# Batch start of a fused attention and feed-forward kernel: who splits the second and third pair, when reciprocals are taken, and when the first batch's value products run

## The chip, the cores and the metric

The kernel runs on one core of one Trainium2 chip. The core has five engines, each with an instruction queue of its own that is worked off in order: TensorE (PE, matrix products and transposes), VectorE (DVE), ScalarE (ACT), GpSimd (POOL) and SyncE (SP, which only starts transfers). The metric is the device time of one execution in microseconds, lower is better. Times are medians over several executions; a profile shows one further execution.

## What is computed

For 8 batches and 8 heads with 576 positions and head size 64, attention with a threshold below the row's largest score, then a feed-forward layer with a leaky rectifier on the joined heads:

```python
scores = scale * np.matmul(q, k.transpose(0, 1, 3, 2))
thresh = np.max(scores, axis=-1, keepdims=True) - tau
scores = np.where(scores >= thresh, scores, -1000000000.0)
scores = scores - np.max(scores, axis=-1, keepdims=True)
attn = np.exp(scores)
attn = attn / (np.sum(attn, axis=-1, keepdims=True) + 1e-09)
attn_out = np.matmul(attn, v)
x = attn_out.transpose(0, 2, 1, 3).reshape(B * S, H * D)
h = x @ w_in                      # 4608 x 512 by 512 x 2048
out = np.maximum(0.01 * h, h) @ w_out
```

## The kernel before

**Steps.** The work of attention is cut into 144 steps, 18 for each batch (`PERB`). A step holds 128 queries of a pair of heads against all 576 keys. The 512 main positions of a batch give two blocks, each of four pairs of heads by two halves `c`; two further steps hold the 64 tail positions of all heads. Two steps (`c` 0 and 1) of the same pair make a `Pair`, whose weights are turned and multiplied with the values together. The first 8 steps are called `early`: their weights are turned on TensorE (`turn_w_pe`), those of all others by a transposing transfer on SyncE's queue (`turn_w`).

**One step.** `scores` (L244) makes the scores of both heads on TensorE into one pair of PSUM tiles `sc`, and there is only one such pair, so that the next step's scores wait for `copy_min`. `copy_min` (L252, VectorE) copies the negated scores out and takes the row minimum. `threshold` adds tau (L261 on VectorE up to step 27, L264 on GpSimd from there). One step later `exps` (ScalarE, L283, L284, L287) makes the exponentials, and `weights` (L296, VectorE) the thresholded weights of head 0. `recip` (L302, VectorE) inverts the sums, `widen` (L305) spreads the result beside the weights so that it is turned along with them. `pv` (L340, TensorE) multiplies turned weights with the values some steps later, `evacuate` (L362 and L352, VectorE) scales and stores the result as input `x` of the layers. It, `pv` and the filler products share one PSUM buffer, "pv". Four pairs make a group of 256 tokens, whose `layer1` units (L383) run one for each step and `layer2` units (L399) two for each step.

**Splitting.** Queries and keys are needed as two half-precision parts, turned so that the head size lies on the partitions. A key such as `(0, 1, "k")` names batch, pair and tensor; `"t"` in place of the pair is the tail. `split_now` rounds to the first part on ScalarE (L157) and takes the rest on VectorE (L158). `split_pool` does all of it on GpSimd: `split_scale` (L137), `split_high` (L143), `split_low` (L147). `turn` (L176) transposes both parts on TensorE into a PSUM tile of the two buffers called "h", and a copy (L187, tails L179 and L184) moves them to SBUF. The buffers for split parts, `half`, are four.

**Order.** The order of the instructions is written out by hand: the loop at the end goes through the steps `n`, and what is put in `loads_at`, `turns_at`, `pool_at`, `rows_at` and `pv_at` is issued at its step, at the place in the step that the loop has. `first` is the list of the first batch's units: pair 0 keys and queries, tail keys, pair 1 keys (`first[3]`) and queries (`first[4]`), pair 2 keys and queries (`first[5]`, `first[6]`), pair 3 keys and queries, tail queries. Pair 0 and the tail keys are split by `split_now` ahead of the loop, pair 1 by `split_now` in step 0, the others by `split_pool`. `idle` (L505) issues filler products on TensorE. Products with the values follow `pv_at`: three steps after the pair's second step where it is early, four in the first batch, five elsewhere. Layer weights are loaded and converted by transfers on GpSimd's queue (`load_w`, L489 and L492).

Of the kernel before, what the change touches and what calls it, by code (L numbers as in the profile page):

```python
# [10 lines left out]
FP16 = mybir.dt.float16  # L11
AX = mybir.AluOpType
# [25 lines left out]
def kernel(  # L38
# [43 lines left out]

    def load_tails(b, which, eng=None):
        t = sb.tile([128, 2, 2, 64], FP32, tag="rawt", bufs=2, name="rawt")
        src = SRC[which][b, :, MAIN:S, :].rearrange("(u sh) p d -> u p sh d", u=2)
        for u in range(2):
            (eng or nc.sync).dma_start(out=t[ds(64 * u, 64), :, :, :].rearrange("p s h d -> p (s h) d"), in_=src[u])
        tails[b, which] = t
# [55 lines left out]

    def split_low(key):
        n = 2 if key[1] == "t" else 4
        nc.gpsimd.tensor_tensor(out=halves[key][:, 1, 0:n, :, :], in0=scaled.pop(key)[:, 0:n, :, :],  # L147
                                in1=halves[key][:, 0, 0:n, :, :], op=AX.subtract)

    def split_now(key):  # L150
        t = halves[key] = new_half()
        for i in range(2):
            if key[1] == "t":
                src, n = tails[key[0], key[2]][:, :, i, :], 2
            else:
                src, n = pair_of(*key)[:, i, :, :], 4
            nc.scalar.activation(out=t[:, 0, 0:n, i, :], in_=src, func=AF.Copy, bias=0.0, scale=64.0)  # L157
            nc.vector.scalar_tensor_tensor(out=t[:, 1, 0:n, i, :], in0=src, scalar=64.0, in1=t[:, 0, 0:n, i, :],  # L158
                                           op0=AX.mult, op1=AX.subtract)

    def turn(key, copy=None):
        copy = copy or nc.scalar.copy
# [14 lines left out]
        if p == "t":  # L177
            for x in range(2):
                copy(out=dst[:, x, :, ds(c0, 64)], in_=tp[:, x, :, :, :].rearrange("d u s p -> d (u s) p"))  # L179
            if which == "k" and b:  # L180
                nc.gpsimd.tensor_copy(out=dst[:, :, :, 576:640], in_=dst[:, :, :, 0:64])
            elif which == "k":
                for x in range(2):
                    nc.vector.tensor_copy(out=dst[:, x, :, 576:640],  # L184
                                          in_=tp[:, x, :, :, :].rearrange("d u s p -> d (u s) p"))
        else:
            copy(out=dst[:, :, p, ds(c0, 512)], in_=tp[:, :, :, :].rearrange("d x t p -> d x (t p)"))  # L187
# [283 lines left out]
    load_pair(0, "q", nc.scalar)  # L471
    load_tails(0, "k", nc.sync)
    load_pair(1, "k", nc.sync)
# [4 lines left out]
    for s in range(2):  # L478
        load_v(0, s)
        if s == 0:  # L480
            load_vtails(0)
    load_tails(0, "q", nc.sync)
    for t in v16:
# [133 lines left out]
```

## Time and profile before

| | us |
|---|---|
| median of 3 runs | 500.47 (500.11 to 500.74) |
| profiled execution | 500.9 |
| its span in the profile | 499.1 |
| TensorE busy | 475.7 (95% of the span) |
| ScalarE busy | 433.1 (87%) |
| VectorE busy | 414.3 (83%) |
| GpSimd busy | 305.5 (61%) |

The span runs from the first to the last instruction; the execution's time has a little around it. Busy times of engines overlap. In a timeline a row is start, duration, engine, line of the kernel, operation, tiles written and read, shape, and in brackets the idle time ahead of it with what ended it. "SPq" and "ACTq" are the queues that start transfers, and "PEld" is TensorE's loading of stationary operands beside its products.

### The profile page before, as it was taken

How to read it: one execution, taken by the hardware profiler on the slowest of the kernel's cores; microseconds unless marked ns; L12 is line 12 of the kernel's file. 1: busy time of each engine (PE TensorE's matmuls, PEld its weight loads, DVE VectorE, ACT ScalarE, POOL GpSimd, SP SyncE). 2: the span in 40 equal slices, each digit the busy share in tenths (PEclk: the TensorE clock that was granted, in tenths of full speed). 3: DMA queues.
4: the chain of work that ended last, by engine and by line, in shares of the span. 5: the costliest groups of instructions: out<-in, count | busy, mean ns of one | idle time of the engine just before them, and what ended most of it. 6: DMA issues, size and time to landing. Idle time of an engine off the chain costs nothing.

```text
span 499.1 us, 19695 instructions
## 1 busy us (share of the span) xinstructions
PE 475.7 (95%) x8043; PEld 344.4 (69%) x8043; DVE 414.3 (83%) x1228; ACT 433.1 (87%) x785; POOL 305.5 (61%) x517
## 2 busy tenths in 40 slices
PE   7878789989999999999999999999999999999996
PEld 6556566656677777777777777777777777667884
DVE  4999999998989898998989898998989898878100
ACT  4998987898999999999999999999999999999431
POOL 4973687557867687666867687666867683322000
PEclk9989999999999999999999999999999999999999
DMA  8897898899998999999997999999898969767512
GB/s 246 238 202 121 156 193 175 144 205 189 217 168 182 193 204 211 186 165 220 191 185 172 203 199 199 195 172 210 197 200 153 205 148 158 138 117 144 126 45 65
DMA packets 220443, 87.79 MB, mean 176 GB/s; under 512 B 190656, under 2 KB 217280, under 8 KB 220352
## 3 DMA queue, kind: packets, MB, share of 16 engines
q1 hardware_dynamic: 217392, 82.07, 80.5%
q0 software_dynamic: 2688, 4.19, 4.8%
q8 instruction: 63, 1.03, 0.9%
q10 hardware_dynamic: 272, 0.26, 0.2%
q14 instruction: 28, 0.23, 0.1%
HBM read 36.70 MB, written 9.44 MB: 92 GB/s over the span
## 4 chain that ended last, share of the span: by engine, by line
PE 80%; DVE 11%; ACT 3%; DMA 2%; issue 1%; POOL 1%; SPq 0%; DVEq 0%; POOLq 0%; ACTq 0%
PE hp L383 26%; PE o L399 20%; PE sc L244 20%; PE pv L340 7%; DVE s L252 5%; PE osc L399 3%; DVE w L296 3%; PE tpr L199 3%; DMA wT<-w 2%; DMA rawt<-in_k_dram 1%; DVE x L362 1%; ACT wT L325 1%; ACT s L283 1%; DVE half L158 1%; ACT e L287 1%
## 5 line engine op out<-in xcount | busy, mean ns | idle before, releaser
L252 DVE TENSOR_SCALAR_CACHE_REDUCE s<-sc 128x576 f32<-128x576 f32 x288 | 206.4, 754 | 32.6 <-PE sc L244 31.4
L244 PE MATMUL sc<-kT,qT 64*128 64x288 f16 (+1 forms) x1920 | 135.8, 286 | 4.0 <-DVE s L252 3.2
L383 PE MATMUL hp<-x,win 128*64 128x256 f16 x2048 | 136.5, 275 | 1.1 <-DVE x L362 1.0
L383 PEld LDWEIGHTS <-win 128*64 128x64 f16 x2560 | 118.5, 109 | 24.0 <-issue 18.1
L399 PE MATMUL o<-wout,g 128*64 128x512 f16 x992 | 127.8, 379 | 0.0
L296 DVE SCALAR_TENSOR_TENSOR w<-s,th,e 128x576 f16<-128x576 f32 x144 | 122.2, 849 | 0.5 <-ACT e L287 0.5
L244 PEld LDWEIGHTS <-qT 64*128 64x128 f16 (+1 forms) x1920 | 77.0, 97 | 58.6 <-issue 44.2
L264 POOL TENSOR_SCALAR th<-mn 128x2 f32<-128x2 f32 x116 | 53.5, 461 | 103.3 <-DVE s L252 76.9
L284 ACT ACTIVATE w<-s,minus_tau 128x576 f16<-128x576 f32 x144 | 111.7, 776 | 5.2
L283 ACT ACTIVATE s<-s,th 128x576 f32<-128x576 f32 x144 | 110.4, 766 | 2.0 <-POOL th L264 1.4
L287 ACT ACTIVATE e<-s,mn 128x576 f16<-128x576 f32 x144 | 110.2, 766 | 0.6 <-DVE s L252 0.5
L385 ACT ACTIVATE g<-hp 128x512 f16<-128x512 f32 x144 | 84.2, 585 | 29.3 <-PE hp L383 28.8
L399 PEld LDWEIGHTS <-g 128*64 128x64 f16 x1152 | 65.1, 110 | 30.1 <-issue 0.5
L147 POOL TENSOR_TENSOR half<-scaled,half 128x512 f16<-128x512 f32 (+1 forms) x75 | 82.2, 1096 | 1.1
L340 PE MATMUL pv<-wT,v 128*64 128x256 f16 (+1 forms) x960 | 52.1, 247 | 2.6 <-DMA wT<-w 2.6
L340 PEld LDWEIGHTS <-v 128*64 128x64 f16 x960 | 41.6, 111 | 15.8 <-issue 3.0
L137 POOL TENSOR_SCALAR scaled<-raw 128x512 f32<-128x512 f32 x60 | 43.7, 728 | 7.1 <-DMA raw<-in_k_dram 6.1
L305 POOL CAST w<-rec 128x256 f16<-128x256 f32 (+1 forms) x70 | 27.9, 398 | 31.4 <-DVE rec L302 31.0
L143 POOL CAST half<-scaled 128x512 f16<-128x512 f32 (+1 forms) x75 | 43.2, 576 | 4.6
L106 POOL CAST v<-vraw 128x256 f16<-128x256 f32 x64 | 34.4, 565 | 1.4
L362 DVE TENSOR_TENSOR x<-pv,wT 128x256 f16<-128x256 f32 x64 | 27.1, 423 | 3.5 <-PE pv L340 3.5
L284 ACT ACTIVATION_READ_ACCUMULATOR w<-s,minus_tau 128x1 f32 x144 | 26.9, 187 | 0.0
(52 smaller groups left out, 327.8 us busy)
## 6 DMA issues: line engine op xcount, KB each, us to landing
vraw<-in_v_dram SPq DMA_DIRECT2D x16, 512.0 KB, 5.4
out_dram<-osb SPq DMA_DIRECT2D x16, 512.0 KB, 3.4
raw<-in_k_dram SPq DMA_DIRECT2D x14, 512.0 KB, 4.7
raw<-in_q_dram SPq DMA_DIRECT2D x14, 512.0 KB, 5.3
win<-in_moe_w_in_dram POOLq DMA_DIRECT2D x4, 512.0 KB, 8.5
wout<-in_moe_w_out_dram POOLq DMA_DIRECT2D x4, 512.0 KB, 12.8
wT<-w SPq DMA_TRANSPOSE x68, 6.0
raw<-in_k_dram SPq DMA_DIRECT2D x4, 256.0 KB, 4.7
```

The source lines that it names most:

```text
L147: nc.gpsimd.tensor_tensor(out=halves[key][:, 1, 0:n, :, :], in0=scaled.pop(key)[:, 0:n, :, :], in1=halves[key][:, 0, 0:n, :, :], op=AX.sub ...
L244: nc.tensor.matmul(out=o, lhsT=lhs, rhs=turned[st.b, "k"][rows, kx, pair, ds(key0, 288)], start=(i == 0), stop=(i == 2), skip_group_check= ...
L252: nc.vector.tensor_scalar(out=st.s[:, h, :].rearrange("p (a b) -> p a b", a=2), in0=st.sc[h][:, :, 0:288], scalar1=-1.0 / UNIT, scalar2=No ...
L264: nc.gpsimd.tensor_scalar(out=st.th[:, :, 0], in0=st.mn[:, :, 0], scalar1=1.0, scalar2=tau_f, op0=AX.mult, op1=AX.add)
L283: nc.scalar.activation(out=z, in_=z, func=AF.Prelu, bias=st.th[:, h, 0:1], scale=-1.0, alpha=1e20)
L284: nc.scalar.activation(out=st.w[h], in_=z, func=AF.Exp, bias=minus_tau[:, :], scale=1.0, accum_out=st.sum[h])
L287: nc.scalar.activation(out=st.e[:, :], in_=st.s[:, h, :], func=AF.Exp, bias=st.mn[:, h, 0:1], scale=-1.0)
L296: nc.vector.scalar_tensor_tensor(out=st.w[0], in0=st.s[:, 0, :], scalar=st.th[:, 0, 0:1], in1=st.e[:, :], op0=AX.is_le, op1=AX.mult, accum ...
L340: nc.tensor.matmul(out=o, lhsT=v16[st.b % 2][:, 2 * c + u if st.tail else st.p, blk, :], rhs=rhs, start=(i == 0), stop=(i == 4), skip_grou ...
L383: nc.tensor.matmul(out=hp[ds(64 * u2, 64), jj, :], lhsT=w_in16[:, i, ds(128 * j + 64 * u2, 64)], rhs=g.x[:, i, :], start=(i == 0), stop=(i ...
L385: nc.scalar.activation(out=g.g[:, ds(nj * u, nj), :], in_=hp[:, :, :], func=AF.Prelu, bias=0.0, scale=1.0, alpha=0.01)
L399: nc.tensor.matmul(out=g.o[ds(64 * u2, 64), :], lhsT=g.g[:, j, ds(128 * m + 64 * u2, 64)], rhs=w_out16[:, j, :], start=(j == 0), stop=(j = ...
```

## The change

1. The first batch's pair 1 is no longer split by ScalarE and VectorE in step 0. Its keys go through `split_pool` ahead of the loop; its queries and the keys of pair 2 get their first part from ScalarE in one instruction (`split_high_act`) and scale and rest from GpSimd. The queries of pair 2 get the same in step 1. The copy of pair 1's turned keys goes from ScalarE to VectorE.
2. `split_low` of batches 0 and 1 is issued as two instructions of half the size.
3. Tails: `split_now` and the copies of `turn` take one instruction where they took two; the second load of the first tail keys goes to ScalarE's queue; the first tail keys are turned into the PSUM buffer "o".
4. Fillers: the `idle(4)` ahead of the tail keys goes; those of steps 5 to 10 stand behind the layer products and ahead of the value products, no longer behind `copy_min`.
5. Pair 3's keys and queries are split in steps 1 and 2 (were 0 and 1), its queries turned in step 5 (was 4); layer weights are loaded from step 0 on (was 2).
6. In steps up to 35 the reciprocal of a pair that isn't early is taken one step later, right behind that step's score copies, and widening and the turning transfer follow behind the threshold.
7. In the first batch the value products of pairs that aren't early come five steps after the pair's second step (was four).

```diff
-    def load_tails(b, which, eng=None):
+    def load_tails(b, which, engs=(nc.sync, nc.sync)):
...
-            (eng or nc.sync).dma_start(out=t[ds(64 * u, 64), :, :, :].rearrange("p s h d -> p (s h) d"), in_=src[u])
+            engs[u].dma_start(out=t[ds(64 * u, 64), :, :, :].rearrange("p s h d -> p (s h) d"), in_=src[u])
...
     def split_low(key):
         n = 2 if key[1] == "t" else 4
-        nc.gpsimd.tensor_tensor(out=halves[key][:, 1, 0:n, :, :], in0=scaled.pop(key)[:, 0:n, :, :],
-                                in1=halves[key][:, 0, 0:n, :, :], op=AX.subtract)
+        m = 2 if key[0] < 2 else n
+        src = scaled.pop(key)
+        for i in range(0, n, m):
+            nc.gpsimd.tensor_tensor(out=halves[key][:, 1, i : i + m, :, :], in0=src[:, i : i + m, :, :],
+                                    in1=halves[key][:, 0, i : i + m, :, :], op=AX.subtract)
+
+    def split_high_act(key):
+        halves[key] = new_half()
+        nc.scalar.activation(out=halves[key][:, 0, :, :, :].rearrange("p t h d -> p h t d"), in_=pair_of(*key),
+                             func=AF.Copy, bias=0.0, scale=64.0)
...
-    def turn(key, copy=None):
+    def turn(key, copy=None, bank="h"):
...
-            tp = ps.tile([128, 2, 2, 2, 64], FP16, tag="h", bufs=2, name="tp")
+            tp = ps.tile([128, 2, 2, 2, 64], FP16, tag=bank, bufs=2 if bank == "h" else 1, name="tp")
...
-    load_tails(0, "k", nc.sync)
+    load_tails(0, "k", (nc.sync, nc.scalar))
...
-    idle(4)
-    turn(first[2])
+    turn(first[2], bank="o")
     idle(5)
-    for key in first[5:7]:
-        split_pool(key)
-    for n_, key in zip((0, 1, 6), first[7:]):
+    split_pool(first[3])
+    for key in first[4:6]:
+        split_high_act(key)
+        split_scale(key)
+        split_low(key)
+    for n_, key in zip((1, 2, 6), first[7:]):
         at(pool_at, n_, lambda key=key: split_pool(key))
     for i in range(8):
-        at(pool_at, 2 + i // 2 if i < 4 else i, lambda i=i: load_w(i))
-    at(turns_at, 0, lambda: turn(first[3]))
-    for n_, key in zip((1, 2, 3, 4, 8), first[5:]):
+        at(pool_at, i if i < 2 else 1 + i // 2 if i < 6 else i, lambda i=i: load_w(i))
+    at(turns_at, 0, lambda: turn(first[3], nc.vector.tensor_copy))
+    for n_, key in zip((1, 2, 3, 5, 8), first[5:]):
...
-    pv_at = {s.n + (3 if s.early else 4 if s.b == 0 else 5): s for s in steps if s.c == 1}
+    pv_at = {s.n + (3 if s.early else 5): s for s in steps if s.c == 1}
+    ended = []
...
             copy_min(steps[n])
+            if ended:
+                recip(ended[0], 0, 2)
         if n == 0:
-            split_now(first[3])
             threshold(steps[0])
-            split_now(first[4])
         if n == 1:
+            split_high_act(first[6])
+            split_scale(first[6])
+            split_low(first[6])
             turn(first[4], nc.vector.tensor_copy)
-        if n < 11:
+        if n < 5:
             idle(8 if n else 16)
...
             threshold(steps[n])
+        if ended:
+            widen(ended[0], 0, 2)
+            turn_w(ended.pop())
...
                 widen(last.pair, last.c, 1, nc.vector if n < 7 else nc.gpsimd)
+            elif last.c == 1 and n < 2 * PERB:
+                ended.append(last.pair)
             elif last.c == 1:
...
                 layer2(n)
+        if 5 <= n < 11:
+            idle(8)
         if n in pv_at:
```

More of the change, by code (lines that the diff above doesn't have):

```diff
@@ L146, in split_low @@
         n = 2 if key[1] == "t" else 4
-        nc.gpsimd.tensor_tensor(out=halves[key][:, 1, 0:n, :, :], in0=scaled.pop(key)[:, 0:n, :, :],
-                                in1=halves[key][:, 0, 0:n, :, :], op=AX.subtract)
+        m = 2 if key[0] < 2 else n
[7 more added lines that the diff above has]
+                             func=AF.Copy, bias=0.0, scale=64.0)
     def split_now(key):
         t = halves[key] = new_half()
-        for i in range(2):
+        for i in range(1 if key[1] == "t" else 2):
             if key[1] == "t":
-                src, n = tails[key[0], key[2]][:, :, i, :], 2
-            else:
[L156 to L159, printed above, removed]
-    def turn(key, copy=None):
+                src = tails[key[0], key[2]][:, :, :, :]
+                hi, lo = (t[:, x, 0:2, :, :] for x in range(2))
+            else:
+                src = pair_of(*key)[:, i, :, :]
+                hi, lo = (t[:, x, :, i, :] for x in range(2))
+            nc.scalar.activation(out=hi, in_=src, func=AF.Copy, bias=0.0, scale=64.0)
+            nc.vector.scalar_tensor_tensor(out=lo, in0=src, scalar=64.0, in1=hi, op0=AX.mult, op1=AX.subtract)
+    def turn(key, copy=None, bank="h"):
         copy = copy or nc.scalar.copy
@@ L177, in turn @@
         if p == "t":
-            for x in range(2):
-                copy(out=dst[:, x, :, ds(c0, 64)], in_=tp[:, x, :, :, :].rearrange("d u s p -> d (u s) p"))
+            src = tp[:, :, :, :, :].rearrange("d x u s p -> d x (u s) p")
+            copy(out=dst[:, :, :, ds(c0, 64)], in_=src)
             if which == "k" and b:
@@ L182, in turn @@
             elif which == "k":
-                for x in range(2):
-                    nc.vector.tensor_copy(out=dst[:, x, :, 576:640],
-                                          in_=tp[:, x, :, :, :].rearrange("d u s p -> d (u s) p"))
+                nc.vector.tensor_copy(out=dst[:, :, :, 576:640], in_=src)
         else:
@@ L481 @@
             load_vtails(0)
-    load_tails(0, "q", nc.sync)
+    load_tails(0, "q")
     for t in v16:
```

## The prediction

> **What bounds the kernel now.** I read the busy times in stretches first, then VectorE's timeline from the start, then what the other engines did where a VectorE row is long or late. In the windows the columns after the length are busy us of TensorE, its weight loads, VectorE, ScalarE, GpSimd, then the granted clock, DMA share and GB/s.
>
> ```profile
> core 0: us, PE busy (x) PEld busy (x) DVE busy (x) ACT busy (x) POOL busy (x), PEclk, DMA share, GB/s
> 20.00:30.00 10.00, 6.96 (x135) 5.40 (x133) 9.52 (x32) 9.85 (x17) 9.70 (x19) 1.00 1.05 233
> 80.00:90.00 10.00, 9.92 (x194) 7.20 (x192) 9.34 (x33) 8.74 (x16) 5.76 (x9) 1.00 0.55 111
> 100.00:110.00 10.00, 8.79 (x133) 5.38 (x131) 9.51 (x32) 9.13 (x17) 6.27 (x10) 1.00 0.86 203
> ```
> ```profile
> 160.00:200.00 40.00, 40.00 (x760) 29.01 (x758) 35.77 (x103) 37.23 (x69) 29.92 (x50) 1.00 0.95 191
> ```
>
> From 160 us on TensorE has no gap: whatever reaches that stage earlier ends earlier by the same amount, as the order of its work there is unchanged. Ahead of it TensorE has holes (3.0 us in ten at 20, 1.2 at 100) while VectorE is at 9.5 of 10. So up to about 70 us, and again near 100 us, a microsecond off VectorE's path is a microsecond off the end; from 80 to 90 TensorE must give it as well.
>
> VectorE's path at the start (start us, duration, engine, line, tile):
>
> ```profile
> 10.19 0.76 DVE L252 TENSOR_SCALAR_CACHE_REDUCE s<-sc 128x576 f32<-128x576 f32 x1 [0.42 <-PE sc L244]
> ...
> 11.55 1.44 DVE L158 SCALAR_TENSOR_TENSOR half<-raw,half 128x256 f16<-128x256 f32 x2
> ...
> 12.98 2.05 DVE L158 SCALAR_TENSOR_TENSOR half<-raw,half 128x256 f16<-128x256 f32 x2
> 14.96 0.74 DVE L252 TENSOR_SCALAR_CACHE_REDUCE s<-sc 128x576 f32<-128x576 f32 x1
> ```
> ```profile
> 12.80 1.21 POOL L147 TENSOR_TENSOR half<-scaled,half 128x512 f16<-128x512 f32 x1
> ```
>
> Score copies of steps 0 and 1 begin at 10.19 and 14.96. Between them stand the four subtractions of the second pair's split, 3.5 us. The first two took 1.44 us; the second two began while GpSimd's 1.21 us subtraction ran, took 2.05 and ended 1 us after it.
>
> **A. Second pair's split off VectorE.** Pieces of the new path:
>
> ```profile
> 1.25 1.41 SPq L87 DMA_DIRECT2D rawt<-in_k_dram  x2
> 2.71 0.61 SPq L467 DMA_DIRECT2D raw<-in_k_dram  x1
> ```
> ```profile
> DMA to landing us min/median/max: 3.4/4.7/5.5
> ```
> ```profile
> 8.85 0.62 POOL L137 TENSOR_SCALAR scaled<-raw 128x512 f32<-128x512 f32 x1 [6.09 <-DMA raw<-in_k_dram]
> 9.53 0.61 POOL L143 CAST half<-scaled 128x512 f16<-128x512 f32 x1
> ...
> 21.70 1.32 POOL L489 DMA_DIRECT2D win<-in_moe_w_in_dram  x2
> ...
> 30.05 0.67 POOL L147 TENSOR_TENSOR half<-scaled,half 128x256 f16<-128x256 f32 x1
> ```
> ```profile
> 8.16 0.41 PE L176 MATMUL tp<-ident,half 128*64 128x128 f16 x8 [0.81 <-ACT kT L187]
> ...
> 10.11 1.07 PE L505 MATMUL idle<-ident 128*128 128x128 f16 x16
> ...
> 15.98 0.64 PE L176 MATMUL tp<-ident,half 128*64 128x128 f16 x16
> ...
> 17.05 0.91 PE L244 MATMUL sc<-kT,qT 64*128 64x288 f16 x12 [0.43 <-DVE qT L187]
> ```
> ```profile
> 8.61 0.65 ACT L179 COPY kT<-tp 128x256 f16<-128x256 f16 x2 [0.50 <-PE tp L176]
> ```
> ```profile
> 9.29 0.49 DVE L184 COPY kT<-tp 128x256 f16<-128x256 f16 x2 [1.15 <-ACT kT L179]
> ...
> 21.40 0.69 DVE L187 COPY qT<-tp 128x1024 f16<-128x1024 f16 x1
> ```
>
> The tail's transposes waited 0.81 us for a PSUM buffer that ScalarE's key copy held; in the bank "o" they don't, so ScalarE's 0.50 us wait goes. Its tail copies, and VectorE's, become one instruction each: about 0.15 off 0.65 + 0.49, an estimate. Score copies of step 0 come 0.65 earlier, at 9.55. The tail's second load issued beside SyncE's queue could add up to 0.7; at these loads' bandwidth I count nothing and keep 0.7 as a bound. Step 1: TensorE ends scores 0 at 9.5, runs the 16 fillers (1.07) to 10.6 and the second pair's key transposes (0.64) to 11.25. GpSimd is idle till then: that pair's load, issued near 2.0 instead of 2.71 (one of the two tail issues ahead of it leaves the queue) and landing within 5.5, is there by 7.5; 0.62 + 0.61 + two halves of 0.67 and small gaps end by 10.3. VectorE copies the keys by 11.95 (0.69), scores 1 end at 12.2 (0.91 and a hand-over). Score copies of step 1 begin at 12.2 instead of 14.96: **-2.75**. From there to step 2 VectorE's list is the old one. The query split by ScalarE's first half and GpSimd's rest ends near 12.4 and is needed when VectorE is through the copies of step 1 at 13.6. Further down GpSimd's line: third-pair keys by 14.5, one weight-load issue (half of 1.32), third-pair queries by 17.3, their transposes by 18.0, their VectorE copy at 21.40 - 2.75 = 18.65. Cover shrinks to 0.7 there; without it each later microsecond of GpSimd is one of VectorE. Bounds: -2.2 (GpSimd 0.5 late) to -3.5.
>
> **B. Steps 4 to 7.** The fourth pair's queries are turned in step 5 instead of 4, the fillers go behind the weight transposes.
>
> ```profile
> 31.32 1.99 DVE L296 SCALAR_TENSOR_TENSOR w<-s,th,e 128x576 f16<-128x576 f32 x1
> ...
> 48.48 0.81 DVE L296 SCALAR_TENSOR_TENSOR w<-s,th,e 128x576 f16<-128x576 f32 x1
> ```
> ```profile
> 31.52 1.17 POOL L147 TENSOR_TENSOR half<-scaled,half 128x512 f16<-128x512 f32 x1
> ```
>
> Step 6 needs those queries and their copy is now VectorE's last work of step 5: scores 6 (0.91) and hand-overs begin only behind it, a stall of 1.1. Against that, the weights of step 5 took 1.99 beside a GpSimd subtraction, 0.81 at 48.48, so 1.18 of blocking. Halved subtractions should leave part: I take half, -0.7. **+0.4**, bounds -0.1 and +1.2. The moved fillers no longer hold up weight transposes, but VectorE wasn't waiting there: 0.
>
> **C. Reciprocals behind the next copies.**
>
> ```profile
> 49.53 0.66 DVE L187 COPY qT<-tp 128x1024 f16<-128x1024 f16 x1
> ...
> 63.72 0.89 DVE L296 SCALAR_TENSOR_TENSOR w<-s,th,e 128x576 f16<-128x576 f32 x1
> ...
> 64.54 0.68 DVE L187 COPY qT<-tp 128x1024 f16<-128x1024 f16 x1
> ```
>
> With a reciprocal between, the query copy begins 0.24 after the end of the weights of 48.48; without one, 0.07 before it: 0.31 per pair. Behind the score copies the reciprocal sits in the gap ahead of the threshold. I take 0.25 for four pairs up to 70 us: **-1.0** (-0.5 to -1.25).
>
> **D. First batch's products one step later.**
>
> ```profile
> 70.42 0.74 PE L340 MATMUL pv<-wT,v 128*64 128x256 f16 x10 [1.54 <-DMA wT<-w]
> ...
> 77.61 0.74 PE L340 MATMUL pv<-wT,v 128*64 128x256 f16 x10 [1.04 <-DMA wT<-w]
> ```
> ```profile
> 72.11 0.76 DVE L252 TENSOR_SCALAR_CACHE_REDUCE s<-sc 128x576 f32<-128x576 f32 x1 [0.29 <-PE sc L244]
> ...
> 79.30 0.76 DVE L252 TENSOR_SCALAR_CACHE_REDUCE s<-sc 128x576 f32<-128x576 f32 x1 [0.49 <-PE sc L244]
> ```
>
> TensorE waited 2.6 us for turned weights; VectorE felt 0.78 of it. The transposes are issued two score copies later (1.5) on SyncE's queue, now behind that step's loads; the products come a step later (72.11 to 79.30 are two, 3.6 each). So 2.1 us is won on waits of 1.54 and 1.04. Five reciprocals (steps 18 to 26) add 1.25 if TensorE keeps up, which it can where its wait and one layer-1 unit leave this stretch. Between 0 and -2.0, nearer the latter: **-1.5**. **E.** Three more pairs near 105 us, where both engines have gaps: **-0.4** (0 to -0.75).
>
> **F. What moves back.** The second group's layers run a step later, so one step's layer-2 work goes from step 27 to 35.
>
> ```profile
> 130.08 0.89 PE L244 MATMUL sc<-kT,qT 64*128 64x288 f16 x11 [0.31 <-DVE s L252]
> ...
> 134.52 1.03 PE L399 MATMUL o<-wout,g 128*64 128x512 f16 x8
> ```
>
> It costs up to 0.9 where TensorE is full; 0.31 of slack and more stands right behind: **+0.4** (0 to +0.9).
>
> The rest is nothing: loads of layer weights start sooner on GpSimd's queue, well ahead of their use; the waits that the new order could lengthen have the covers named.
>
> ```profile
> span 499.1 us, 19695 instructions
> ```
>
> Sum: -2.75 + 0.4 - 1.0 - 1.5 - 0.4 + 0.4 = -4.85. The profiled execution took 500.9 (this span and 1.8 around it); the median of the runs shown is 500.47, 0.43 less. 500.9 - 4.85 - 0.43 = **495.6**.
>
> **The rivals.** *GpSimd blocks VectorE (slower).* By the rows of A GpSimd splits for 13.6 us up to the fourth pair (three full splits of 2.57, three of 1.96 without the first half) where it took 4 x 2.4 = 9.6, so 4 us more, beside VectorE's weights.
>
> ```profile
> 16.98 0.96 DVE L296 SCALAR_TENSOR_TENSOR w<-s,th,e 128x576 f16<-128x576 f32 x1
> ```
>
> For it: the 2.05 and 1.99 rows. Against: with GpSimd at 9.7 of 10 the weights at 16.98 still took only 0.96, 0.15 over 0.81. If each of the 17 weights up to step 17 waited out one half subtraction (0.67), 17 x 0.67 = 11.4, less the 1.18 and 0.15 paid in the rows shown, is +10.1: 505.7. It turns the sign when the mean block grows by 4.85 / 17 = 0.29.
>
> [...]
>
> *Transposes still late.* If SyncE's queue, whose transposes landed 4.9 to 8.3 us after issue, eats the won 2.1 us, D and E go:
>
> ```profile
> DMA to landing us min/median/max: 4.9/5.8/8.3
> ```
>
> For it: batch 1's products get no extra step while its transposes also start 1.5 later. Against: the median of 5.8 beside the three steps, over 10 us at the pace of D, from issue to use. 495.6 + 1.9 = 497.5.
>
> *The start is lost to loads.* The DMA share is 1.05 at 20 to 30 us; if the early weight loads push back raw loads, or GpSimd's longer line delays the third pair by 2.3 us, most of A goes: 497.9. Against it:
>
> ```profile
> 40.11 0.29 POOL L305 CAST w<-rec 128x128 f16<-128x128 f32 x1 [4.87 <-DVE rec L302]
> ```
>
> GpSimd had 4.87 us to spare before 40 us, so only the first 25 us can suffer.
>
> **How the numbers follow.** Forecast 0.53, late transposes 0.15, lost start 0.10, blocking 0.22. Within 0.2% (1.0 us, what a measurement here can tell from none) falls the mild part of blocking, 0.08; its rest, 0.14, is slower; faster 0.78. The range adds the bounds: -3.5 - 0.1 - 1.25 - 2.0 - 0.75 + 0 = -7.6 gives 492.9; -2.2 + 1.2 - 0.5 + 0 + 0 + 0.9 = -0.6 gives 499.9. It holds the two middle rivals and leaves out the slower one.
>
> **What would show it.** Right: score copies of step 1 near 12.2 and of step 8 near 37.5 us; a VectorE gap near 1.1 ahead of step 6's copies; no product waiting for turned weights near 70 to 80; TensorE full from a point some 5 us earlier. Wrong: weights rows of 1.2 us or more repeated through the first 60 us, product waits of 1 us in steps 18 to 34, score copies of step 3 waiting behind late third-pair queries, or a lowered clock over step 6's scores.

## The result and the profile after

The changed kernel takes 495.76 us (median of four runs, 495.05 to 497.21) where the kernel before, beside it on the same chip, takes 500.61 (500.11 to 500.81): a ratio of 0.9908 with an interval of 0.9882 to 0.9934. The forecast was 495.6. The profiled execution took 495.05, its span is 493.2 where it was 499.1, so this one shows 5.9 us of gain where the medians show 4.85. The top of the page of the changed kernel:

```profile
span 493.2 us, 19697 instructions
...
PE 476.3 (97%) x8039; PEld 344.5 (70%) x8039; DVE 408.8 (83%) x1220; ACT 431.3 (87%) x781; POOL 316.3 (64%) x534
...
PE 82%; DVE 4%; ACT 1%; issue 1%; DVEq 0%
```

TensorE's work is the same 476 us, and its share rose only because the span shrank. VectorE has 5.5 us less to do, GpSimd 10.8 more. Ten-microsecond stretches of the changed kernel, and the later one in which TensorE was full already (same columns as before):

```profile
20.00:30.00 10.00, 7.06 (x136) 5.20 (x138) 9.04 (x33) 9.93 (x18) 9.69 (x18) 1.00 0.94 217
30.00:40.00 10.00, 9.00 (x140) 6.57 (x136) 8.31 (x28) 8.54 (x16) 9.69 (x16) 0.83 1.12 214
...
80.00:90.00 10.00, 10.00 (x202) 7.52 (x198) 9.28 (x31) 9.73 (x18) 6.81 (x12) 1.00 0.93 182
...
100.00:110.00 10.00, 9.62 (x142) 5.85 (x140) 9.40 (x31) 9.10 (x18) 8.06 (x12) 1.00 0.93 187
```
```profile
160.00:200.00 40.00, 40.00 (x728) 28.98 (x726) 35.77 (x103) 37.20 (x68) 29.50 (x51) 1.00 0.98 203
```

The hole near 100 us shrank from 1.2 to 0.4, the one at 20 did not (7.06 of ten, 6.96 before): there a new wait stands, which follows below. From 160 on TensorE is as full as it was, and the lead over the kernel before, 6.13 us at step 40, is 6.14 at the last step too. The gain is therefore made early, and the start of each step's score copies shows where (start in us, and the change against before):

| step | 0 | 1 | 2 | 4 | 6 | 8 | 17 | 26 | 31 | 37 |
|---|---|---|---|---|---|---|---|---|---|---|
| before | 10.19 | 14.96 | 18.41 | 25.62 | 33.78 | 39.88 | 69.03 | 98.35 | 112.88 | 131.32 |
| after | 9.23 | 11.66 | 15.51 | 22.36 | 30.68 | 37.62 | 65.33 | 93.01 | 106.62 | 125.20 |
| change | -0.96 | -3.30 | -2.90 | -3.26 | -3.10 | -2.26 | -3.70 | -5.34 | -6.26 | -6.12 |

VectorE's timeline of the changed kernel, around step 1, steps 5 to 7, and the first pair whose reciprocal is late:

```profile
9.23 0.76 DVE L260 TENSOR_SCALAR_CACHE_REDUCE s<-sc 128x576 f32<-128x576 f32 x1 [0.61 <-PE sc L252]
...
10.83 0.69 DVE L195 COPY kT<-tp 128x1024 f16<-128x1024 f16 x1
11.66 0.76 DVE L260 TENSOR_SCALAR_CACHE_REDUCE s<-sc 128x576 f32<-128x576 f32 x1
...
27.59 0.81 DVE L304 SCALAR_TENSOR_TENSOR w<-s,th,e 128x576 f16<-128x576 f32 x1
...
28.71 0.53 DVE L313 CAST w<-rec 128x128 f16<-128x128 f32 x1
29.00 0.68 DVE L195 COPY qT<-tp 128x1024 f16<-128x1024 f16 x1
30.68 0.76 DVE L260 TENSOR_SCALAR_CACHE_REDUCE s<-sc 128x576 f32<-128x576 f32 x1 [1.00 <-PE sc L252]
...
34.99 0.76 DVE L260 TENSOR_SCALAR_CACHE_REDUCE s<-sc 128x576 f32<-128x576 f32 x1 [0.67 <-PE sc L252]
...
45.96 0.81 DVE L304 SCALAR_TENSOR_TENSOR w<-s,th,e 128x576 f16<-128x576 f32 x1
...
46.70 0.69 DVE L195 COPY qT<-tp 128x1024 f16<-128x1024 f16 x1
...
48.98 0.17 DVE L310 RECIPROCAL rec<-sum 128x4 f32<-128x4 f32 x1
49.10 0.15 DVE L269 TENSOR_SCALAR_CACHE_REDUCE th<-mn 128x2 f32<-128x2 f32 x1
```

Between the copies of steps 0 and 1 only the threshold and one copy of 0.69 us are left. The weights issued in step 5 took 0.81 at 27.59, where the kernel before had 1.99 at 31.32. Ahead of step 6 the stall stands as forecast, 1.00 us behind the moved query copy, and the step after it waits 0.67 more. At 46.70 the query copy starts without a reciprocal ahead of it, which now sits at 48.98 ahead of the threshold. TensorE's timeline of the changed kernel shows the wait at 20 to 30 us from the other side, and the one product that still waits for turned weights:

```profile
29.74 0.91 PE L252 MATMUL sc<-kT,qT 64*128 64x288 f16 x12 [2.35 <-DVE qT L195]
...
31.48 1.03 PE L513 MATMUL idle<-ident 128*128 128x128 f16 x8
32.57 1.28 PE L348 MATMUL pv<-wT,v 128*64 128x256 f16 x10
...
57.01 0.74 PE L348 MATMUL pv<-wT,v 128*64 128x256 f16 x10 [0.84 <-DMA wT<-w]
```

The eight fillers take 1.03 and the products 1.28 behind the gap of 2.35, where 0.62 and 0.74 are usual: the granted clock halves, as the two-microsecond stretches of the same kernel say (TensorE's clock is the third number from the end):

```profile
28.00:30.00 2.00, 0.26 (x6) 0.22 (x8) 1.54 (x5) 2.00 (x4) 2.00 (x5) 1.00 1.00 194
30.00:32.00 2.00, 2.00 (x38) 1.54 (x33) 1.32 (x3) 1.97 (x5) 1.94 (x5) 0.74 1.04 206
32.00:34.00 2.00, 1.94 (x19) 1.33 (x19) 1.83 (x10) 1.97 (x4) 1.85 (x3) 0.50 1.01 190
34.00:36.00 2.00, 2.00 (x40) 1.52 (x36) 1.33 (x4) 0.64 (x3) 1.97 (x4) 0.91 1.11 228
```

### The profile page after: what moved, and what is told of

Read it like the earlier page. It is cut to its first block, busy times and chain, and to the rows that moved or that the text cites. A ratio compares the mean times of both kernels' runs of the same rounds, so it can differ in the third digit from the quotient of the medians.

```text
span 493.2 us, 19697 instructions
## 1 busy us (share of the span) xinstructions
PE 476.3 (97%) x8039; PEld 344.5 (70%) x8039; DVE 408.8 (83%) x1220; ACT 431.3 (87%) x781; POOL 316.3 (64%) x534
## 3 DMA queue, kind: packets, MB, share of 16 engines
q8 instruction: 63, 1.03, 0.9%
## 4 chain that ended last, share of the span: by engine, by line
PE 82%; DVE 4%; ACT 1%; issue 1%; DVEq 0%
PE hp L391 27%; PE o L407 21%; PE sc L252 21%; PE pv L348 7%; PE osc L407 4%; PE tpr L207 3%; DVE s L260 2%; DVE w L304 1%; DVE x L370 0%; PE tp L186 0%; ACT w L292 0%; ACT s L291 0%; ACT e L295 0%; ACT g L393 0%; ACT osb L413 0%
## 5 line engine op out<-in xcount | busy, mean ns | idle before, releaser
L304 DVE SCALAR_TENSOR_TENSOR w<-s,th,e 128x576 f16<-128x576 f32 x144 | 120.5, 837 | 0.5 <-ACT e L295 0.5
L151 POOL TENSOR_TENSOR half<-scaled,half 128x512 f16<-128x512 f32 (+1 forms) x91 | 90.2, 998 | 2.0
L143 POOL CAST half<-scaled 128x512 f16<-128x512 f32 (+1 forms) x74 | 44.3, 599 | 4.5
L313 POOL CAST w<-rec 128x256 f16<-128x256 f32 (+1 forms) x70 | 32.1, 459 | 15.9 <-DVE rec L310 4.6
L106 POOL CAST v<-vraw 128x256 f16<-128x256 f32 x64 | 31.3, 520 | 1.3
## 6 DMA issues: line engine op xcount, KB each, us to landing
wout<-in_moe_w_out_dram POOLq DMA_DIRECT2D x4, 512.0 KB, 10.3
```

Source lines behind the costliest of these rows:

```text
L151: nc.gpsimd.tensor_tensor(out=halves[key][:, 1, i : i + m, :, :], in0=src[:, i : i + m, :, :], in1=halves[key][:, 0, i : i + m, :, :], op= ...
L304: nc.vector.scalar_tensor_tensor(out=st.w[0], in0=st.s[:, 0, :], scalar=st.th[:, 0, 0:1], in1=st.e[:, :], op0=AX.is_le, op1=AX.mult, accum ...
```

## The experiments

Each kernel was timed beside the kernel before on the same chip, whose median was 500.57, 500.63 and 500.81 us in the three batches. Where a step is said to start earlier or later, to lead or to lose, its score copies are meant, against the kernel before, in the experiment's own profile.

**The late half alone.** The kernel before, with only points 6 and 7 of the change.

```diff
-    pv_at = {s.n + (3 if s.early else 4 if s.b == 0 else 5): s for s in steps if s.c == 1}
+    pv_at = {s.n + (3 if s.early else 5): s for s in steps if s.c == 1}
+    ended = []
...
+            if ended:
+                recip(ended[0], 0, 2)
...
+        if ended:
+            widen(ended[0], 0, 2)
+            turn_w(ended.pop())
```

> The kernel before with points 6 and 7 of the change alone (late reciprocals, products five steps late). My theory: the two parts of the change add, so this one brings C, D, E and F of the prediction, -1.0 - 1.5 - 0.4 + 0.4 = -2.5 us, a ratio near 0.995; score copies of step 8 at the old 39.9 us, those of step 26 some 2.5 to 3 us before the old 98.35, no product waiting 1 us for turned weights. Rival, transposes still late: only C, -1.0 us or less, with product waits near 70 and 77 us still there.

Measured 498.33 (497.82 to 498.45), ratio 0.9955 [0.9940, 0.9970]. Its copies start 0.51 later than before at step 8, 0.53 earlier at step 17, 1.68 at step 26, 2.58 at step 31, 2.44 at step 37. At step 26 a lead of 2.5 to 3 was expected; 0.64 is lost in step 3, where a widening cast took 1.16 us that took 0.47 in the profile before, though the instructions up to there are the same in both. Products wait for turned weights once, 0.89 us.

**The start alone.** The changed kernel, with points 6 and 7 taken back.

```diff
-    pv_at = {s.n + (3 if s.early else 5): s for s in steps if s.c == 1}
+    pv_at = {s.n + (3 if s.early else 4 if s.b == 0 else 5): s for s in steps if s.c == 1}
...
-            if ended:
-                recip(ended[0], 0, 2)
...
-        if ended:
-            widen(ended[0], 0, 2)
-            turn_w(ended.pop())
...
-            elif last.c == 1 and n < 2 * PERB:
-                ended.append(last.pair)
```

> The changed kernel with points 6 and 7 undone (reciprocal in the same step, first batch's products four steps late). My theory: A and B alone, -2.35 us by the prediction and -2.3 to -2.9 by the step times of the changed kernel's trace, a ratio near 0.9950; score copies of step 8 near 37.6 us and waits for turned weights of 1 to 1.5 us back near 67 and 75 us. Rival, the start is lost downstream: step 8 early all the same, but step 26 within 1 us of the old 98.35 and a ratio of 0.998 or more.

Measured 498.39 (497.88 to 498.65), ratio 0.9957 [0.9942, 0.9971]. The two halves give 2.24 and 2.18 us, together 4.42 of the 4.85: they add, within the scatter of the runs. In its profile step 4 starts 3.87 earlier, step 8 only 1.05: the loss in steps 5 to 7 is far larger than in the changed kernel's profile. VectorE's timeline of this kernel has the reason:

```profile
30.78 0.76 DVE L260 TENSOR_SCALAR_CACHE_REDUCE s<-sc 128x576 f32<-128x576 f32 x1 [1.71 <-PE sc L252]
...
33.78 1.85 DVE L313 CAST w<-rec 128x128 f16<-128x128 f32 x1
35.55 0.48 DVE L333 COPY wT<-wp 128x640 f16<-128x640 f16 x1
```

The half clock fell on the scores themselves (1.62 instead of 0.91), so the stall is 1.71; and the widening of the same step, 0.23 in the changed kernel, took 1.85. GpSimd's timeline of this kernel shows what ran beside it:

```profile
33.65 1.31 POOL L151 TENSOR_TENSOR half<-scaled,half 128x256 f16<-128x256 f32 x2
34.93 0.61 POOL L137 TENSOR_SCALAR scaled<-raw 128x512 f32<-128x512 f32 x1
```

The two halves of a subtraction stand back to back with the next split's scale behind them; the cast began 0.13 later and was done 0.09 after the scale. The held cast is the larger part: from step 6 to 7 this kernel loses 1.95, the changed kernel 0.76. Between steps 8 and 26 it then wins 1.5 more, which the sum did not give to the start; its products wait 0.41 and 1.04 us for turned weights, where those of the kernel before wait 1.54 and 1.04.

**The late reciprocals without the extra step.** The changed kernel, with point 7 alone taken back.

```diff
-    pv_at = {s.n + (3 if s.early else 5): s for s in steps if s.c == 1}
+    pv_at = {s.n + (3 if s.early else 4 if s.b == 0 else 5): s for s in steps if s.c == 1}
```

> The changed kernel with the first batch's products four steps late again, reciprocals still late. My theory: transposes start 1.5 us later than in the kernel before and the products have no more room, so the waits of 1.5 and 1.0 us grow to 2 us and more on three or four pairs between 55 and 85 us, and the kernel loses D and some: +1.5 to +3 us, 497.3 to 498.8. Rival, the extra step is not what pays: within 0.5 us of the changed kernel.

Measured 500.97 (499.08 to 502.56), ratio 1.0009 [0.9991, 1.0027]: the whole gain is gone, 5.2 us against the changed kernel, more than expected. TensorE's timeline of this kernel, in an execution of 499.69:

```profile
57.12 0.74 PE L348 MATMUL pv<-wT,v 128*64 128x256 f16 x10 [3.03 <-DMA wT<-w]
57.78 1.58 PE L252 MATMUL sc<-kT,qT 64*128 64x288 f16 x12
...
69.82 0.74 PE L348 MATMUL pv<-wT,v 128*64 128x256 f16 x10 [0.96 <-DMA wT<-w]
...
77.40 0.74 PE L348 MATMUL pv<-wT,v 128*64 128x256 f16 x10 [1.43 <-DMA wT<-w]
```

Three waits of 5.4 us together, where the kernel before had two of 2.6. The first is the first pair that a transfer turns, and the 3.03 us gap halves the clock behind it (scores in 1.58): from step 13 to 14 the lead falls from 3.34 to 0.12. So late reciprocals without the extra step are a loss here: the start alone, which has neither, took 498.39. The extra step without late reciprocals was not run, so how the gain of the late half is shared between the two is not shown by a time.

**Whole subtractions.** The changed kernel, with point 2 taken back.

```diff
-        m = 2 if key[0] < 2 else n
+        m = n
```

> The changed kernel with GpSimd's subtractions whole again. If a VectorE instruction with two SBUF inputs waits out the GpSimd instruction it meets, blocks of up to 1.2 us come back among the weights of steps 0 to 17, whose mean rises from about 0.89 to 0.95 us or more: +0.5 to +1.5 us, 496.3 to 497.3. Rival, the halving is worth nothing, since the blocks are mostly by other GpSimd work: within 0.3 us of the changed kernel (it costs GpSimd about 0.14 us a subtraction, which could also make whole ones faster by some tenths).

Measured 496.42 (496.14 to 496.54), ratio 0.9918 [0.9903, 0.9932]. That is 0.66 above the changed kernel, with overlapping intervals, and within what was expected. What halving does to VectorE can be read directly. The weights of the first batch, by durations, in the kernel before, in the changed one and in this one (minimum, median and maximum in ns):

```profile
L296 DVE SCALAR_TENSOR_TENSOR w<-s,th,e x17: 814/894/1986, 17.0 to 70.6; 128x576 f16<-128x576 f32 x17
```
```profile
L304 DVE SCALAR_TENSOR_TENSOR w<-s,th,e x17: 812/815/1314, 13.7 to 66.9; 128x576 f16<-128x576 f32 x17
```
```profile
L304 DVE SCALAR_TENSOR_TENSOR w<-s,th,e x17: 814/933/1553, 13.3 to 68.2; 128x576 f16<-128x576 f32 x17
```

The means are 1.00, 0.91 and 1.04 us, so against whole subtractions halving takes some 2 us of waiting off these 17. Little of that reaches the end: in its profile this kernel loses 3.3 us from step 4 to 8, in the stall of step 6 and behind it, and wins 3.61 from step 8 to 37, where the changed kernel wins 3.85. Halving is thus not shown to be worth the 0.66; most of what the profile loses stands in the stall.

**The tail keys' path as before.** The changed kernel, with point 3 and the fillers ahead of the tail keys taken back; the instructions of `split_now` and of the tails' copies are two again.

```diff
-    load_tails(0, "k", (nc.sync, nc.scalar))
+    load_tails(0, "k")
...
-    turn(first[2], bank="o")
+    idle(4)
+    turn(first[2])
```

> The changed kernel with the tail keys' path as before: both loads on SyncE's queue, four fillers and a wait for the shared buffer ahead of their transposes, two instructions for each split and copy. The prediction gave these parts 0.65 of A's 2.75 us. Theory: score copies of step 0 go back from 9.23 to some 10.0 us and all behind them with it: +0.5 to +0.9 us, about 496.5. Rival: GpSimd's split of the second pair, not step 0, sets step 1, so that it stays near 11.7 us and the time near 495.8.

Measured 498.75 (five runs from 498.64 to 499.45, one of 496.26), ratio 0.9947 [0.9926, 0.9968], 3.2 above the changed kernel in the same batch: far more than expected. But its first steps don't show 3.2. Copies of step 0 start at 10.05, those of step 2 at 15.79, and the changed kernel's second profile has 15.80 there: the late tail keys are made up for within two steps. At step 4 the two are level still, and at step 8 this one is 1.8 behind. That comes in steps 6 and 7, again in VectorE's timeline (of this kernel, whose lines are one further):

```profile
31.64 0.76 DVE L261 TENSOR_SCALAR_CACHE_REDUCE s<-sc 128x576 f32<-128x576 f32 x1 [1.71 <-PE sc L253]
...
33.20 1.11 DVE L305 SCALAR_TENSOR_TENSOR w<-s,th,e 128x576 f16<-128x576 f32 x1
...
34.62 1.84 DVE L314 CAST w<-rec 128x128 f16<-128x128 f32 x1
```

It is the pattern of the start alone: the half clock falls on all of the scores (1.62 us where 0.91 is usual), the step shifts, and the widening cast lands behind a pair of half subtractions (on GpSimd from 34.50, scale from 35.77 to 36.38). A further 1.4 goes between steps 37 and 100 (the lead falls from 3.74 to 2.37), where the instructions are those of the changed kernel and every other kernel here keeps its lead within 0.03; its cause is not shown. That point 3 is worth 3.2 us does not follow. What it shows is that the stall of step 6 costs between 1 and 3 us, by what happens to stand beside it.

**Fillers in the stall.** The changed kernel, with 44 fillers instead of 8 in step 5, to keep TensorE busy while it waits for the queries.

```diff
-            idle(8)
+            idle(44 if n == 5 else 8)
```

> The changed kernel with 36 more filler products in step 5, in the 2.35 us in which TensorE waits for the fourth pair's query copy. In the changed kernel's trace the granted clock is 0.74 and 0.50 from 30 to 34 us, right behind that gap, and VectorE then waits 0.67 us for the scores of step 7. If the gap is what lowers the clock, it stays at 1.00 from 30 to 34 us, the 0.67 us wait goes and step 8 comes 0.5 to 0.9 us earlier: about 495.0. Rival, the clock falls whatever fills that gap, or the wait is not the clock's: step 8 and the time as in the changed kernel, 495.8.

Measured 496.54 (494.38, 496.57, 496.51, 496.95), ratio 0.9907 [0.9885, 0.9929]. In its profile, which is the execution of 494.38, the clock stays at 1.00 through these steps and the wait at step 7 is gone; step 8 starts at 36.41 where the changed kernel has 37.62. But the three other runs are no better than the changed kernel. The mechanism is seen in one profile, the gain in time is not.

**Fillers in their old place.** The changed kernel, with point 4's move of the fillers of steps 5 to 10 taken back.

```diff
-        if n < 5:
+        if n < 11:
             idle(8 if n else 16)
...
-        if 5 <= n < 11:
-            idle(8)
```

> The changed kernel with the fillers of steps 5 to 10 back behind the score copies. The prediction gave their move nothing. Theory: they wait for the shared buffer up to 1.9 us with the weight transposes behind them, and ScalarE's copies later, but VectorE isn't reached: within 0.5 us of the changed kernel. Rival, ScalarE is full near 20 to 30 us (9.9 of 10), so late copies reach VectorE: +1 us or more, with VectorE waiting for ScalarE near 25 to 45 us.

Measured 494.80 (494.46 to 495.25), ratio 0.9881 [0.9867, 0.9896]. Moving the fillers brought nothing: by the medians it costs 0.8 to 1.0 us, more than the 0.5 that was expected at most, but the intervals overlap. In this profile TensorE's wait for the queries is 1.83 us and the clock stays at 1.00.

**The fourth pair's queries turned where they were.** The changed kernel, with that turn in step 4 again.

```diff
-    for n_, key in zip((1, 2, 3, 5, 8), first[5:]):
+    for n_, key in zip((1, 2, 3, 4, 8), first[5:]):
```

> The changed kernel with the fourth pair's queries turned in step 4 as before. In the changed kernel's trace TensorE waits for that split until 25.97 us, in step 5. Theory: GpSimd is the later one, so TensorE, in step 4 near 23 us, stands 2 to 3 us before the transposes with the scores of step 5 behind it: the 1.0 us stall at step 6 goes, a stall of 1.5 to 3 us at step 5 comes, +0.5 to +2 us, 496.3 to 497.8. Rival, the stall at step 6 was an avoidable loss: -1.0 us, 494.8.

Measured 496.22 (495.35 to 497.37), ratio 0.9903 [0.9887, 0.9920]: no gain. The stall moves a step ahead, because GpSimd has not split those queries by then. TensorE waits 1.66 us for it (and 0.76 and 0.35 for the two halves), and step 5 starts 1.62 earlier than before instead of 3.74. The profile is of the slowest run, 497.37; in it the lead falls from 2.14 at step 6 to nothing at step 7, where a widening cast took 1.84. Point 5 followed from GpSimd's longer line and was not the cause of the stall.

**Those queries split first.** As the last, but GpSimd splits them ahead of the value conversions of step 2, and the products of early pairs come four steps after the pair's second step, not three.

```diff
+    pool_at[2].insert(0, pool_at[2].pop())
...
-    pv_at = {s.n + (3 if s.early else 5): s for s in steps if s.c == 1}
+    pv_at = {s.n + (4 if s.early else 5): s for s in steps if s.c == 1}
```

> A version that may beat both: on GpSimd the fourth pair's queries are split ahead of the first value casts (2.3 us sooner, near 23.7 us), turned in step 4, and the value products of the early pairs run one step later, so that the casts are in time. Theory: the 1.0 us stall ahead of step 6 and TensorE's 2.35 us gap go, and with the gap the lowered clock: step 8 comes 1.0 to 1.7 us earlier than in the changed kernel, 494.1 to 494.8. Rival, the first group's layer work, one step later, is missed elsewhere or ScalarE holds: no gain, 495.8 or more.

Measured 495.03 (494.93 to 495.50), ratio 0.9887 [0.9872, 0.9902], a little above what was expected. No stall ahead of step 6, clock at 1.00, step 8 3.21 earlier than before. Later it gives back 0.5 at step 23 and 0.6 at step 27 against the changed kernel, where VectorE waits 0.49 and 0.48 us for scores; that this comes from layer work a step later is argued, not shown.

**The changed kernel once more, and two better orders.** The changed kernel unchanged; the last with four steps for the products of the first pair alone; and the same with the fillers in their old place.

```diff
-    pv_at = {s.n + (4 if s.early else 5): s for s in steps if s.c == 1}
+    pv_at = {s.n + (4 if s.n == 1 else 3 if s.early else 5): s for s in steps if s.c == 1}
```

> The changed kernel itself, once more, beside the next three: its own spread is the question, since its four runs lay from 495.05 to 497.21 while two versions of it had theirs within 0.8 us. Theory: the lowered clock near 30 us depends on where the gaps of TensorE fall, and a run shows it or not: 495 to 497 again, median near 495.8. Rival: those two long runs were chance, all runs within 0.8 us of 495.1.

> The version with the fourth pair's queries split ahead of the value casts and turned in step 4, with only the first pair's value products a step later. The version with all early products a step later lost 0.4 us at step 23 and 0.4 at step 27 against the changed kernel, where its layer work came a step late. Theory: those 0.8 us are not lost here, the rest of the gain stays (step 8 near 36.7 us): 494.2 to 494.8, runs within 0.8 us. Rival: products of the second pair, which need casts that now come later, wait: 495.0 or more.

> The same with the fillers back behind the score copies. Theory: with no stall left in steps 5 and 6 their place is worth nothing, within 0.4 us of the version before it. Rival: the old place keeps the clock up by itself and is 0.5 us or more faster, or, with the products moved, they wait longer for the shared buffer and cost 0.5 us or more.

| | us | ratio to before |
|---|---|---|
| changed kernel | 495.59 (494.31 to 496.30) | 0.9888 [0.9868, 0.9907] |
| queries first, one pair late | 494.42 (493.78 to 494.63) | 0.9865 [0.9847, 0.9882] |
| the same, fillers as before | 494.28 (494.11 to 494.62) | 0.9865 [0.9845, 0.9884] |

Both beat the kernel before. Against the changed kernel they are 1.2 and 1.3 us lower by the medians, with runs that touch only at 494.31 to 494.63, but the intervals of the ratios overlap. In the profile of the second the clock halves behind a gap of 2.29 us, and its time is 494.36 all the same. In both the widening of step 5 took 1.52, so that a held cast stands where the stall was. TensorE's timeline of the first of the two, where the changed kernel has its 2.35 us gap:

```profile
25.53 0.62 PE L513 MATMUL idle<-ident 128*128 128x128 f16 x8
26.21 0.74 PE L348 MATMUL pv<-wT,v 128*64 128x256 f16 x10
26.88 0.91 PE L252 MATMUL sc<-kT,qT 64*128 64x288 f16 x12
27.91 0.69 PE L331 MATMUL wp<-ident,w 128*64 128x128 f16 x18
```

The scores of step 6 follow at once, and step 8 starts at 36.32, 3.56 earlier than before.

## Why the prediction was right, and where it was not

The sum was -4.85, and the medians moved by 4.85. That they agree to the last digit is luck: the changed kernel run again gained 5.22, its ten runs lie 2.9 us apart, and single terms are off by up to 0.6 either way. The mechanism holds: the late half and the start, each tried alone, give what the terms gave them (2.24 and 2.18; the terms D, E, F and C sum to -2.5, A and B to -2.35). The profiled execution is 1 us better than its sum, so its terms come out larger than forecast.

*A, second pair's split off VectorE, -2.75 by step 1.* Measured -3.30 by step 1, -2.90 by step 2. The chain went as described: GpSimd's two half subtractions (1.30 us from 8.88) were over at 10.18 for a forecast of 10.3. What is more is there at step 0 already, which starts 0.96 earlier, not 0.65: the tail's second load was counted as nothing, with 0.7 kept as a bound. ScalarE's split of the tail keys waited for that load in the kernel before and doesn't in the changed one:

```profile
6.70 0.51 ACT L157 ACTIVATE half<-rawt 128x128 f16<-128x128 f32 x2 [1.18 <-DMA rawt<-in_k_dram]
```
```profile
5.93 0.40 ACT L168 ACTIVATE half<-rawt 128x256 f16<-128x256 f32 x1
```

How much of it shows hangs on when the first loads land: step 0 starts between 8.45 and 9.23 in the eleven profiles with the changed kernel's opening, 1.0 to 1.7 earlier than before. From step 1 to 2 the profile loses 0.40, which A had at nothing: weights of 1.06 for 0.96 and a widening of 0.52 for 0.24. The cover of 0.7 for the third pair's queries held, as step 3 starts 2.85 earlier, where step 2 has 2.90.

*B, steps 4 to 7, +0.4.* Steps 4 to 8 lost 1.00 us in the profile (-3.26 to -2.26), inside the bounds but mis-sized. The stall was 1.00 for 1.1, and the block on step 5's weights went altogether (1.99 to 0.81, -1.18 where -0.7 was taken as half; half of 1.18 is 0.59). What the term lacked is what stands behind the stall: 0.67 us of wait at step 7, under the half clock, and 0.3 on a blocked widening (0.53 where 0.23 is usual); the last 0.2 is a wait of step 4's reciprocal for ScalarE. A lowered clock over these scores was named as what would show the step wrong, but had no price; in this profile it begins just behind them (0.50 from 30.95 us). The runs show that this is the dearest unknown of the case: the same stall costs 1.00 here, 2.82 in the start alone and 2.76 with the old tail path. All three run the same instructions in these steps, so the price hangs on where the half clock and GpSimd's next split fall.

*C, reciprocals, -1.0 for four pairs.* The late half alone gains 1.04 from step 8 to 17. The changed kernel gains 1.44 there, but the start alone, which has no late reciprocal, gains 0.65 as well, so only part of the 1.44 is C.

*D, -1.5.* Measured -1.64 in the changed kernel from step 17 to 26, -1.15 in the late half alone; as the start alone gains 0.87 there too, D is nearer 1 than 1.5. The forecast that no product would wait near 70 to 80 us held; one waits 0.84 us at 57, at the first pair that a transfer turns. *E, -0.4.* Measured -0.92 and -0.90, beyond the bound of -0.75. *F, +0.4.* Measured +0.14 from step 31 to 37. From step 8 to 37 the changed kernel wins 3.85 and the start alone 1.49, so the four terms bring 2.4 there, for a forecast of 2.5.

*The rivals.* GpSimd blocking VectorE does not grow among the weights: the median took 815 ns where it took 894, and the largest 1314 where it took 1986. Whole subtractions show it half alive (933, 1553), at a price in time that is not shown. The widening casts are held as well: 0.52 and 0.53 in the changed kernel, one of 0.47 in the kernel before and of 1.16 in the late half alone, and 1.51 to 1.85 in six of the others. That a half blocks for no longer than its own 0.67 was the author's estimate; in the changed kernel the weights stay within it (1314 less 812 is 0.50). Those with 44 fillers and with the fillers in their old place do not: there one took 1.75, 0.94 more than 0.81, beside a widening cast of 0.30 and a half of 0.68 in a row on GpSimd. The cast of 1.85 in the start alone was held for 1.6 us (1.85 less 0.23), longer than any one GpSimd instruction beside it (two halves of 1.31 together, a scale of 0.61), so work in a row on GpSimd was not broken at its first end. In these rows a half's length bounds the block among the changed kernel's weights, and not where GpSimd's instructions stand in a row.

Late transposes did not come true with the extra step, and did in full without it: 5.2 us, by three waits and a half clock that the forecast of 1.9 for this rival had left out. The start was not lost to loads: step 4 starts 3.26 earlier.

What stays open is the scatter. The changed kernel's runs lie over 494.31 to 497.21, and a trace was kept of single executions only. That the runs differ by how the stall of step 6 falls would fit all profiles, but is not shown for the others; the run of 494.38 with fillers in the stall and its three neighbours near 496.6 are the plainest sign that something there goes one way or another. Each run's mean granted clock is on record, and it does not sort the changed kernel's runs: 0.994 at 494.31 and 0.995 at 497.21. The time at half clock is thus not the whole of it.

## What to carry to other kernels

Work moved to an engine with time to spare gains what it takes off the bound engine, if its own line is followed to the point where its results are needed: here each split was early enough except one, and that one set the only new stall. Issuing a transfer later to clear the way of a busy engine pays only if its consumer is moved along; alone it cost all of the gain (5.2 us). A stall of the matrix engine should be priced with the clock behind it (here 0.50 for 3.4 us or more behind most of them) and with what it shifts the next instructions into; its position, not only its length, decided what it cost here (steps 4 to 8 lost 1.00 us in one profile, 2.82 in another).

## What was not expected of the hardware

The granted clock fell from 1.00 to 0.50 around most gaps of TensorE of about 2 us or more. All waits of 1.8 us or more between 5 and 150 us in the profiles of all kernels here, with the clock in the five microseconds from the gap's end:

| kernel | gap, us | clock by the microsecond |
|---|---|---|
| fillers in old place | 1.83 | 1.00 1.00 1.00 1.00 1.00 |
| before | 1.91 | 0.96 0.50 0.50 0.50 0.84 |
| late half alone | 1.92 | 1.00 1.00 1.00 1.00 1.00 |
| queries first, fillers as before | 2.29 | 0.50 0.50 0.50 0.81 1.00 |
| old tail path | 2.34 | 0.50 0.50 0.50 0.50 0.50 |
| start alone | 2.35 | 0.50 0.50 0.50 0.96 1.00 |
| changed | 2.35 | 1.00 0.60 0.50 0.50 0.69 |
| changed, again | 2.35 | 0.72 0.50 0.50 0.58 1.00 |
| extra step taken back | 2.35 | 0.82 0.50 0.50 0.50 0.97 |
| extra step taken back | 3.03 | 0.87 0.50 0.50 0.50 0.92 |
| whole subtractions | 3.28 | 0.50 0.50 0.50 0.50 0.50 |

Nine waits of 1.30 to 1.66 us kept 1.00; one of 1.45, with the fourth pair's queries turned in step 4, was followed by 0.50; of the two microseconds from 34.00, which reach into that gap, TensorE worked 0.90. So the kernel before paid for its gap too. By the table half speed sets in between the gap's end and 1.2 us behind it, at the same length of gap (2.35 us), and that decided whether the first or the later instructions ran at half speed.

The length of the gap does not sort these rows, but the traces hold what does. Where both ends can be read ahead of 150 us, the half clock lasted 3.40 to 3.42 us, seven times in six profiles. The two falls of the clock with the extra step taken back lie 27.31 us apart, eight times 3.41. In the idle end of the trace it falls once more, in the changed kernel at 491.75 and in the kernel before at 498.44: 460.80 us behind the first fall and 467.62, which is 135 and 137 times 3.413. Where these stretches lie differs between executions: the changed kernel's first fall is at 30.95 in one profile, at 30.46 in the other. In eight profiles an end of the half clock can be read ahead of 150 us, nine ends in all. With stretches of 3.41 us laid from those, TensorE was busy for 0.74 to 1.52 us in the nine ahead of the half clock, and for 1.86 or more in every other one from 5 to 146 us. Stretches of the changed kernel, of the old tail path, where the half clock lasted for two of them, and of the fillers in their old place, where 1.72 kept 1.00 (TensorE's busy time is the second number, the clock the third from the end):

```profile
27.54:30.95 3.41, 1.21 (x26) 0.88 (x28) 2.27 (x8) 3.38 (x7) 3.41 (x8) 1.00 1.03 193
30.95:34.36 3.41, 3.35 (x38) 2.48 (x34) 3.20 (x12) 3.05 (x7) 3.20 (x6) 0.50 1.00 191
34.36:37.78 3.42, 3.34 (x67) 2.37 (x64) 2.65 (x10) 2.39 (x4) 3.33 (x5) 1.00 1.17 240
```
```profile
25.79:29.21 3.42, 1.52 (x36) 1.15 (x32) 3.25 (x12) 3.39 (x7) 3.42 (x7) 1.00 0.82 196
29.21:32.62 3.41, 2.64 (x32) 1.76 (x32) 1.70 (x5) 2.40 (x5) 3.28 (x9) 0.50 1.06 209
32.62:36.03 3.41, 3.35 (x32) 2.36 (x30) 3.24 (x8) 2.60 (x5) 3.30 (x6) 0.50 1.07 210
36.03:39.44 3.41, 2.80 (x48) 1.94 (x44) 3.38 (x11) 2.58 (x4) 1.74 (x3) 1.00 1.23 229
```
```profile
25.64:29.05 3.41, 1.72 (x44) 1.45 (x43) 3.24 (x11) 3.38 (x7) 3.41 (x8) 1.00 0.76 174
29.05:32.46 3.41, 3.27 (x62) 2.48 (x62) 2.38 (x9) 2.93 (x7) 3.28 (x7) 1.00 1.04 214
```

So in these traces a gap was followed by half clock where one stretch held enough of it. The 1.91 us of the kernel before lie within one stretch (27.41 to 30.82, busy 1.50). The 1.92 of the late half alone kept 1.00; an edge at 29.38 would part them into two stretches with 2.19 and 2.38, but the clock shows no edge there, so that this spared it is the author's estimate.
